# Tails of a head pair in one matmul, column tiles for the token-mix tails, a first batch mixed in channel halves, and a new order of steps

## The chip, the cores and the metric

The kernel runs on one core of a Trainium2 chip. Its time is the device time of one execution, in microseconds (us). The kernel before takes 309.3 us, the median of five runs (308.6 to 313.53).

The engines have short names here: PE is TensorE (matmuls), DVE is VectorE, ACT is ScalarE, POOL is GpSimd, and SP is SyncE, which here only issues transfers. Each works through its own list of instructions in order; semaphores hold an instruction back until its inputs and its buffers are ready.

## The reference

There are 8 batches. First comes attention with random features (8 heads, 576 positions, head size 64, 128 features), then a mixer of two two-layer networks over a width of 512:

```python
def phi(x):                                   # x: q or k, scaled
    h = einsum('bhsd,md->bhsm', x, omega) - sum(x * x, -1) / 2
    return exp(h - max(h, -1)) / sqrt(m)
kv  = einsum('bhsm,bhsd->bhmd', phi(k), v)
z   = sum(phi(k), 2)
att = einsum('bhsm,bhmd->bhsd', phi(q), kv) / (einsum('bhsm,bhm->bhs', phi(q), z) + 1e-6)
x   = att as (batch, 576, 512)
u   = x + (relu(x.T @ w_tok1) @ w_tok2).T     # token mixing, 576 -> 256 -> 576
out = u + relu(u @ w_ch1) @ w_ch2             # channel mixing, 512 -> 1536 -> 512
```

## The kernel before

**Tiling.** A batch's 576 positions are split into a main part of 512, in four tiles of 128 (`NJ`), and a tail of 64 (`ST`). All matmul operands are fp16 and sums are fp32 in PSUM. Heads go in four pairs (`hp`), since two heads' tails or two row halves of 64 fill 128 partitions.

**Attention, batch b.** `proj` computes the features of q and k of one head pair: eight matmuls of 128 columns (L338) and two of 512 (L346), all with 64 rows, so that two of them use the two row halves of the array. `proj_exp` takes the exponentials on ACT (L275). The subtraction of the row's square cancels in the quotient, apart from the k maximum: `k_max` finds a maximum per key on DVE (L362, L366), takes its reciprocal into the last column of `v_sc` and scales v with it on POOL (L374). `kv` sums keys times values over the main part in eight matmuls of 65 columns (L388) and the tail in two of 130 columns (L393). `num` and `norm` give the quotient (L414, L422, L423).

**Tails.** `k_tail` copies the 32-column tails of all heads together (L292), makes two matmuls against `bd`, a matrix with omega twice on its diagonal (L296), and one exponential. A tile of the result holds four heads in groups of 32 partitions and one of two interleaved positions, so `k_tail_max` works in four groups of 32 partitions (L317 on DVE, L318 on POOL), and `kv` needs two matmuls for a pair's 64 tail positions. `num_tail` writes the tails of two batches into the two halves of one tile `xt`.

**Mixing.** `tok1` and `tok2` are the token network, for one of two hidden tiles and one of four position tiles (L459, L462, L475). `tok2_tail` does it for the 64-position tails of two batches in four matmuls: `w2t` holds the weights twice, padded with zeros, so that one batch lands in output rows 0 to 63 and the other in 64 to 127 (L486). `u` must be transposed for the channel network: `tokT` does it on PE for batches 0 and 1 (L498), `u_write` and `load_uT` through DRAM and a transposing DMA for the others (L511, L518). `ch1` is one of twelve hidden tiles of the channel network (four matmuls of 512 columns, L530, and a relu on ACT, L537), `ch2` one of four output tiles (twelve matmuls, L542, an addition on DVE, L551, and the output transfer, L553 to L558). The collected tails of all batches are treated as a ninth batch, 8.

**Loading.** q and k of batches 0 and 1 arrive in natural layout, cast to fp16 by POOL's transfers, and are transposed on PE (`t_main` L259, `t_tail` L271, copied out at L262 and L272). From batch 2 on `cast_dram` writes a fp16 copy to DRAM (POOL's queue, L89), which `load_T_v` reads with transposing DMAs on SP's queue (L97). `load_v_all` brings v and its tail (L115, L124).

**PSUM.** There are eight banks: four for attention (`att_ps`), two for `kv` and `num` (`kn_ps`), two for mixing (`mix_ps`). A new tile of a group waits until the tile that had its bank last has been read.

**Order.** The order of all steps is a string, `order` (L569), written out by hand: the program walks through it and issues each step's instructions, each on its engine's list. Nothing reorders them afterwards. Two tables go with it: `SWAP` moves single copies or multiplications to another engine, and `HEAT` puts dummy matmuls (operand `warm`) in front of named steps at the start. The step `ch1 0 0` is the first of the channel network; `tok2 7 0` is the token network of the last batch.

Of the kernel before, what the change touches and what calls it, by code (L numbers as in the profile page):

```python
# [17 lines left out]
def kernel(  # L18
# [54 lines left out]
    HEAT = {('kv', 0, 2): 1, ('kv', 1, 0): 3, ('kv', 1, 1): 2, ('num', 0, 0): 1, ('num', 0, 3): 1, ('num', 0, 4): 1, ('num', 0, 7): 1, ('proj', 0, 1): 1, ('proj', 1, 2): 4, ('t', 0, 0, 'q'): 3, ('t', 0, 4, 'k'): 2, ('t', 0, 6, 'k'): 4, ('t', 0, 6, 'q'): 3}  # L73
    SWAP = {('c', 'q'), ('kv', 0, 3), ('kv', 1, 0), ('r1', 0, 0), ('r1', 0, 1), ('r1', 1, 1), ('t', 0, 2, 'k'), ('t', 0, 6, 'k'), ('t', 0, 6, 'q'), ('t', 1, 0, 'k'), ('t', 1, 0, 'q'), ('t', 1, 4, 'q'), ('tt', 1, 'q'), ('uT', 0, 1), ('uT', 1, 0), ('uT', 1, 1), ('uT', 1, 2), ('uT', 1, 3), ('v', 0, 2), ('v', 1, 3), None}
# [45 lines left out]
    def load_v_tail(b):  # L120
        t = ldpool.tile([P, 4, D], FP32, name="v_tail", tag="v_tail", bufs=1)
        live["vt", b] = t
        for hh in range(4):
            nc.sync.dma_start(  # L124
                out=t[32 * hh : 32 * hh + 32].rearrange("c (g w) d -> c g (w d)", g=2),
                in_=v[b, hh::4, SM:S, :].rearrange("g (c w) d -> c g (w d)", w=2),
            )
# [66 lines left out]
    w2t = wpool.tile([P, NT, 2, P], FP16, name="w2t")  # L194
# [5 lines left out]
    vz = [wpool.tile([P, 4, 4, 72], FP16, name=f"vz{i}") for i in range(2)]  # L200

    for t in (w1t, bd, *vz, *xt, w2t):
        nc.vector.memset(t, 0.0)
# [9 lines left out]
    nc.tensor.transpose(om_ps, omega_nat, ident16)  # L213
    nc.vector.tensor_copy(out=bd[0:D, 0:M], in_=om_ps[0:D, :])
# [33 lines left out]
    def t_main(b, h0, n, which):  # L248
# [18 lines left out]
    def t_tail(b, which):  # L267
        nt = live[which + "natt", b]
        ps = att_ps([P, H, ST // 2], FP16, "tt_ps")
        for h in range(H):  # L270
            nc.tensor.transpose(ps[:, h, :], nt[:, h, :], ident16[0 : ST // 2, 0 : ST // 2])  # L271
        copy_on(False, "tt", b, which)(out=live[which + "T", b][:, :, NP2:SP2], in_=ps)  # L272
# [16 lines left out]
    def k_tail(b):  # L289
        sb = live["kT", b]  # L290
        kt = apool.tile([P, H, ST // 2], FP16, name="k_tt", tag="k_tt")
        (nc.vector if b < 2 else nc.gpsimd).tensor_copy(out=kt, in_=sb[:, :, NP2:SP2])  # L292
        live["kpt", b] = apool.tile([P, 4, M], FP16, name="k_pt", tag="k_pt")
        ps = att_ps([P, 4, M], FP32, "kt_ps")
        for g in range(2):
            nc.tensor.matmul(  # L296
                ps[:, 2 * g : 2 * g + 2, :],
                kt[:, 4 * g : 4 * g + 4, :].rearrange("r h c -> r (h c)"),
                bd,
                start=True,  # L300
                stop=True,
            )
        exp(live["kpt", b], ps)

    def k_tail_max(b):
        kp = live["kpt", b]
        tmp = apool.tile([P, 4, M // 2], FP16, name="mxt", tag="mxt")
# [3 lines left out]
        mx = apool.tile([P, 4], FP16, name="kmt", tag="kmt")  # L311
        nc.vector.reduce_max(out=mx, in_=tmp, axis=AX.X)
        vs = vz[b % 2]
        for hh in range(4):
            r = slice(32 * hh, 32 * hh + 32)
            with nc.allow_low_precision(reason="fp16 operand of the matmul"):
                nc.vector.reciprocal(out=vs[r, hh, :, D], in_=mx[r])  # L317
            nc.gpsimd.tensor_tensor(  # L318
                out=vs[r, hh, :, 0:D],
                in0=live["vt", b][r],  # L320
                in1=vs[r, hh, :, D : D + 1].broadcast_to((32, 4, D)),
# [59 lines left out]
    def kv(b, hp):  # L381
# [9 lines left out]
        g, h0 = hp // 2, (hp % 2) * 2  # L391
        for w in range(2):
            nc.tensor.matmul(  # L393
                ps,
                live["kpt", b][:, 2 * g + w, :],
                vz[b % 2][:, h0 : h0 + 2, 2 * g + w, 0 : D + 1],
                start=False,
                stop=(w == 1),
            )
# [54 lines left out]
    def tok1(b, tb):  # L454
        if tb == 0:
            live["r1", b] = mpool.tile([P, NT, DM], FP16, name="r1", tag="r1")
        ps = mix_ps([P, DM], FP32, "h1_ps")
        for j in range(NJ):
            nc.tensor.matmul(  # L459
                ps, w1m[:, j, tb * P : (tb + 1) * P], live["x", b][:, j, :], start=(j == 0), stop=False  # L460
            )
        nc.tensor.matmul(  # L462
            ps, w1t[:, b % 2, tb * P : (tb + 1) * P], xt[(b // 2) % 2], start=False, stop=True
        )
        if (tb == 0) != (("r1", b, tb) in SWAP):
            nc.scalar.activation(out=live["r1", b][:, tb, :], in_=ps, func=AF.Relu)
        else:
            nc.vector.tensor_relu(out=live["r1", b][:, tb, :], in_=ps)  # L468

    def tok2(b, j):  # L470
        if j == 0:
            live["u", b] = mpool.tile([P, NJ, DM], FP16, name="um", tag="um")
        ps = mix_ps([P, DM], FP32, "ht_ps")
        for tb in range(NT):
            nc.tensor.matmul(  # L475
                ps, w2m[:, tb, j, :], live["r1", b][:, tb, :], start=(tb == 0), stop=(tb == NT - 1)
            )
        nc.vector.tensor_tensor(  # L478
            out=live["u", b][:, j, :], in0=live["x", b][:, j, :], in1=ps, op=ALU.add
        )  # L480

    def tok2_tail(pair):
        ps = mix_ps([P, DM], FP32, "htt_ps")
        for o in range(2):
            for tb in range(NT):
                nc.tensor.matmul(  # L486
                    ps,
                    w2t[:, tb, o, :],
                    live["r1", 2 * pair + o][:, tb, :],
                    start=(o == 0 and tb == 0),  # L490
                    stop=(o == 1 and tb == NT - 1),
# [3 lines left out]
    def u_transpose(src, dst, *key):  # L495
        ps = mix_ps([P, ND, P], FP16, "uT_ps")
        for db in range(ND):
            nc.tensor.transpose(ps[:, db, :], src[:, db * P : (db + 1) * P], ident16)  # L498
        copy_on(False, "uT", *key)(out=dst, in_=ps)

    def tokT(b, j):
        if j == 0:
            live["uT", b] = mpool.tile([P, ND, NJ, P], FP16, name="uT", tag="uT")
        u_transpose(live["u", b][:, j, :], live["uT", b][:, :, j, :], b, j)
# [34 lines left out]
    def ch2(c, j):  # L539
        ps = mix_ps([P, DM], FP32, "h2_ps")  # L540
        for cb in range(NCB):
# [3 lines left out]
                wc2[:, cb, :],  # L545
# [3 lines left out]
        o = opool.tile([P, DM], FP32, name="o_sb", tag="o_sb")  # L549
        u = live["u", c][:, j, :] if c < B else ut[j]  # L550
        nc.vector.tensor_tensor(out=o, in0=u, in1=ps, op=ALU.add)  # L551
        if c < B:
            nc.sync.dma_start(  # L553
                out=out[c, 0:SM, :].rearrange("(p j) d -> p j d", j=NJ)[:, j, :], in_=o
            )
        else:
            nc.sync.dma_start(out=out[2 * j, SM:S, :], in_=o[0:ST])
            nc.sync.dma_start(out=out[2 * j + 1, SM:S, :], in_=o[ST:P])  # L558
# [6 lines left out]
    def load_v_all(b):  # L565
# [4 lines left out]
        load_nat 1 0 4 k; load_nat 1 0 4 q; cast_qk k; load_nat 1 4 8 k; cast_qk q; t_main 0 0 2 q;  # L570
        load_nat_tail 1 k; t_main 0 2 2 q; t_main 0 0 2 k; t_main 0 2 2 k; t_tail 0 k; proj 0 0; proj_exp 0 0
        1; proj_exp 0 0 0; k_tail 0; load_v_tail 1; k_tail_max 0; proj_exp 0 0 2; t_main 0 4 2 k; proj_exp 0 0
        3; k_max 0 0; proj 0 1; proj_exp 0 1 2; proj_exp 0 1 0; load_nat 1 4 8 q; proj_exp 0 1 1; t_main 0 4 2
        q; t_main 0 6 2 k; proj 0 2; proj_exp 0 1 3; proj_exp 0 2 0; proj_exp 0 2 1; kv 0 0; k_max 0 1;
        proj_exp 0 2 2; num 0 0 0; t_tail 0 q; load_wtok; norm 0 0 0; t_main 0 6 2 q; kv 0 1; k_max 0 2; proj
        0 3; proj_exp 0 2 3; num 0 1 1; norm 0 1 1; proj_exp 0 3 0; proj_exp 0 3 1; cast_dram 2 k; proj_exp 0
        3 3; num 0 1 0; t_main 1 0 4 k; t_main 1 0 4 q; num 0 0 1; norm 0 1 0; proj_exp 0 3 2; q_tail 0; k_max
        0 3; kv 0 2; t_tail 1 k; proj 1 0; load_v 1; proj_exp 1 0 0; load_wc1 0; proj_exp 1 0 1; load_nat_tail
        1 q; norm 0 0 1; num 0 2 0; k_tail 1; t_main 1 4 4 k; norm 0 2 0; permute_w2 0; k_tail_max 1; kv 0 3;
        t_main 1 4 4 q; permute_w2 1; cast_dram 2 q; num 0 3 1; proj 1 1; norm 0 3 1; k_max 1 0; proj_exp 1 0  # L580
        2; proj_exp 1 0 3; proj_exp 1 1 0; proj_exp 1 1 1; num 0 3 0; num 0 2 1; proj_exp 1 1 2; norm 0 2 1;
# [113 lines left out]
```

The softmax here doesn't subtract the row's maximum and nothing guards it: scores larger than these inputs give would overflow.

## Time and profile before

| | |
|---|---|
| median of five runs | 309.3 us |
| the profiled execution | 308.6 us |
| its span, first to last instruction | 306.8 us |
| PE clock granted | 0.998 |
| DMA | 46.12 MB, 78,971 packets, mean 150 GB/s |
| instructions | 5,665 |

The span is what the profile's views cover; the profiled execution's own time is 1.8 us longer. A row of the page or of a list of groups names line, engine, operation, the tiles it writes and reads, its shape and how often it occurs; behind the bar stand busy time, mean duration in ns, and the idle time of the engine just before it with what ended it. A timeline row gives start and duration in us. Durations of matmuls are booked longer than their pace, since they overlap; what a matmul costs in a row of them is the distance between starts.

### The profile page before, as it was taken

Reading aid. Unit: us, or ns where it says so; the run is one execution under the profiler, and the core shown is the slowest. Engines: PE = TensorE matmul, PEld = TensorE weight load, DVE = VectorE, ACT = ScalarE, POOL = GpSimd, SP = SyncE. Lnnn points to the kernel's source line nnn. Section 1 sums busy time; section 2 is a strip of 40 time slices with the busy share of each in tenths; the row PEclk is TensorE's granted clock in tenths of the full one; section 3 lists DMA queues with packets and bytes.
Section 4 is the critical chain, followed back from the end, with each engine's and each line's share of the span. In section 5 each row is a group of like instructions: output and inputs, shape, how many; then the busy total and the mean of one; then the engine's idle time right before and its main releaser. Section 6 shows DMA issues by size and latency. Waiting matters only on the chain.

```text
span 306.8 us, 5665 instructions
## 1 busy us (share of the span) xinstructions
PE 290.5 (95%) x2180; PEld 143.1 (47%) x2180; DVE 162.0 (53%) x418; ACT 157.4 (51%) x305; POOL 79.3 (26%) x115
## 2 busy tenths in 40 slices
PE   6788899999999999999999999999999999999993
PEld 2454354455544544544454545545544444444441
DVE  5588984764587686446553458547733421021021
ACT  2779457944956447743673278437633134503500
POOL 9677612611261261115220042105200000000000
PEclk9999999999999999999999999999999999999999
DMA  8999989999989989987969996350232142433021
GB/s 150 187 163 158 203 119 221 227 209 163 288 129 214 269 146 193 251 163 160 213 126 177 238 247 184 91 151 25 85 109 80 71 104 101 57 91 80 2 102 69
DMA packets 78971, 46.12 MB, mean 150 GB/s; under 512 B 46816, under 2 KB 73824, under 8 KB 78560
## 3 DMA queue, kind: packets, MB, share of 16 engines
q1 hardware_dynamic: 68000, 31.50, 44.3%
q0 software_dynamic: 10672, 13.99, 28.5%
q8 instruction: 17, 0.28, 0.4%
q10 hardware_dynamic: 272, 0.26, 0.2%
q14 instruction: 10, 0.08, 0.1%
HBM read 35.88 MB, written 20.19 MB: 183 GB/s over the span
## 4 chain that ended last, share of the span: by engine, by line
PE 74%; DVE 12%; DMA 6%; POOL 2%; ACT 2%; issue 1%; SPq 1%; DVEq 0%; POOLq 0%
PE h_ps L530 28%; PE h_ps L542 26%; PE ht_ps L475 4%; PE h_ps L459 3%; DMA uT<-u 2%; DVE km L366 2%; PE num_ps L414 2%; PE k_ps L338 2%; DMA v_nat<-in_v_dram 2%; PE kv_ps L388 2%; DVE xm L423 2%; DMA q_nat<-in_q_dram 2%; DVE mx L362 2%; PE q_ps L346 2%; PE htt_ps L486 1%
## 5 line engine op out<-in xcount | busy, mean ns | idle before, releaser
L537 ACT ACTIVATE r<-h_ps 128x512 f16<-128x512 f32 x108 | 64.7, 599 | 71.8 <-PE h_ps L530 71.6
L542 PE MATMUL h_ps<-wc,r 128*128 128x512 f16 x432 | 97.0, 379 | 0.0
L530 PE MATMUL h_ps<-uT,wc 128*128 128x512 f16 x384 | 90.7, 379 | 0.6 <-DMA uT<-u 0.5
L542 PEld LDWEIGHTS <-r 128*128 128x128 f16 x432 | 41.2, 98 | 47.4 <-ACT r L537 0.3
L530 PEld LDWEIGHTS <-wc 128*128 128x128 f16 x432 | 40.0, 97 | 43.6 <-issue 2.0
L551 DVE TENSOR_TENSOR o_sb<-um,h_ps 128x512 f32<-128x512 f16 x32 | 22.0, 687 | 60.6 <-PE h_ps L542 60.5
L374 POOL TENSOR_TENSOR v_sc<-v_nat,v_sc 128x512 f16<-128x512 f32 x24 | 25.4, 1057 | 100.3 <-DVE v_sc L370 34.2
L275 ACT ACTIVATE k_p<-k_ps 128x512 f16<-128x512 f32 x64 | 37.0, 605 | 12.6 <-PE k_ps L338 10.0
L275 ACT ACTIVATE q_p<-q_ps 128x512 f16<-128x512 f32 x64 | 37.5, 604 | 4.5 <-PE q_ps L346 4.3
L478 DVE TENSOR_TENSOR um<-xm,ht_ps 128x512 f16<-128x512 f16 x32 | 21.6, 684 | 15.8 <-PE ht_ps L475 15.1
L423 DVE TENSOR_TENSOR xm<-num_ps,rc 128x256 f16<-128x256 f32 x64 | 27.2, 425 | 2.2
L318 POOL TENSOR_TENSOR vz<-v_tail,vz 32x256 f16<-32x256 f32 x32 | 20.3, 635 | 22.2 <-DVE vz L317 15.6
L366 DVE TENSOR_REDUCE km<-mx 128x8 f16<-128x512 f16 x32 | 21.9, 686 | 1.1
L475 PE MATMUL ht_ps<-r,w2m 128*128 128x512 f16 x64 | 18.9, 380 | 2.0 <-DVE r L468 1.0
L414 PEld LDWEIGHTS <-q_p 128*128 128x128 f16 x256 | 14.3, 98 | 13.6 <-issue 3.0
L362 DVE TENSOR_TENSOR mx<-k_p 128x512 f16<-128x512 f16 x32 | 16.2, 505 | 4.5 <-ACT k_p L275 4.2
L414 PE MATMUL num_ps<-kv_sb,q_p 128*128 128x65 f16 x256 | 17.0, 194 | 1.3 <-DVE kv_sb L401 1.2
L459 PE MATMUL h_ps<-xm,w1m 128*128 128x512 f16 x64 | 16.4, 380 | 0.6 <-DVE xm L423 0.6
L422 DVE RECIPROCAL rc<-num_ps 128x4 f32<-128x4 f32 x64 | 10.8, 169 | 10.5 <-PE num_ps L414 10.2
L401 ACT CAST kv_sb<-kv_ps 128x130 f16<-128x130 f32 x30 | 8.2, 272 | 14.1 <-PE kv_ps L393 14.0
L346 PE MATMUL q_ps<-qT,bd 64*128 64x512 f16 x64 | 14.4, 376 | 0.6 <-ACT q_p L275 0.3
L388 PEld LDWEIGHTS <-k_p 128*128 128x128 f16 x256 | 11.4, 98 | 6.7 <-issue 2.0
(97 smaller groups left out, 244.8 us busy)
## 6 DMA issues: line engine op xcount, KB each, us to landing
out_dram<-o_sb SPq DMA_DIRECT2D x32, 256.0 KB, 2.8
v_nat<-in_v_dram SPq DMA_DIRECT2D x12, 512.0 KB, 5.8
k<-in_k_dram POOLq DMA_DIRECT2D x6, 576.0 KB, 7.9
q<-in_q_dram POOLq DMA_DIRECT2D x6, 576.0 KB, 6.8
wc<-in_moe_w_ch_dram POOLq DMA_DIRECT2D x4, 768.0 KB, 9.2
u<-um SPq DMA_DIRECT2D x24, 128.0 KB, 2.1
v_tail<-in_v_dram SPq DMA_DIRECT2D x32, 32.0 KB, 4.5
out_dram<-o_sb SPq DMA_DIRECT2D x8, 128.0 KB, 2.3
```

Of the source, the lines that this page charges most:

```text
L275: nc.scalar.activation(out=out, in_=in_, func=AF.Exp, bias=0.0, scale=c_scale)
L362: nc.vector.tensor_tensor(out=tmp, in0=kp[:, :, 0 : M // 2], in1=kp[:, :, M // 2 : M], op=ALU.max)
L366: nc.vector.reduce_max(out=mx, in_=tmp, axis=AX.X)
L374: (nc.vector if ("v", b, hp) in SWAP else nc.gpsimd).tensor_tensor(out=vs[:, :, 0:D], in0=live["v", b][:, 2 * hp : 2 * hp + 2].rearrange(" ...
L414: nc.tensor.matmul(ps[:, j, :], live["qp", b, hp][:, j % 2, i, j // 2, :], sb, start=True, stop=True)
L423: nc.vector.tensor_tensor(out=live["x", b][:, :, h * D : (h + 1) * D], in0=ps[:, :, 0:D], in1=rc.unsqueeze(2).broadcast_to((P, NJ, D)), op ...
L459: nc.tensor.matmul(ps, w1m[:, j, tb * P : (tb + 1) * P], live["x", b][:, j, :], start=(j == 0), stop=False)
L475: nc.tensor.matmul(ps, w2m[:, tb, j, :], live["r1", b][:, tb, :], start=(tb == 0), stop=(tb == NT - 1))
L530: nc.tensor.matmul(ps, wc1[:, db, cb * P : (cb + 1) * P], uT[:, db].rearrange("p j c -> p (j c)"), start=(db == 0), stop=(db == ND - 1),)
L537: nc.scalar.activation(out=live["r3", c][:, cb, :], in_=ps, func=AF.Relu)
L542: nc.tensor.matmul(ps, live["r3", c][:, cb, j * P : (j + 1) * P], wc2[:, cb, :], start=(cb == 0), stop=(cb == NCB - 1),)
L551: nc.vector.tensor_tensor(out=o, in0=u, in1=ps, op=ALU.add)
```

## The change

Six things change.

- Key tails: the tail tile of a head pair now holds both heads and both interleaved positions (`kt`, with zeros between), against `om2`, which is omega twice, one above the other. A pair's tail is one matmul of 128 columns in `k_tail` and one of 130 columns in `kv`. `k_tail_max` works in two groups of 64 partitions. `load_v_tail` brings v in the order that goes with it.
- Token-mix tails: `tok2_tail` writes each batch to its own 64 output rows with unpadded weights, alternating between the two; `w2t` and its copies go.
- `tok1`, `tok2`, `tokT` and `ch2` can do one half of the 512 channels. The order uses it for the token mixing of batch 0 and for `ch2 8 3`.
- `t_main` and `t_tail` of batch 0 use the mixing banks instead of the attention banks.
- In the half-width `ch2 8 3 1` one of the two output transfers is issued by ACT.
- `order`, `HEAT` and `SWAP` are new throughout.

```diff
     def load_v_tail(b):
-        for hh in range(4):
+        for r in range(4):
+            i, w = r // 2, r % 2
             nc.sync.dma_start(
-                out=t[32 * hh : 32 * hh + 32].rearrange("c (g w) d -> c g (w d)", g=2),
-                in_=v[b, hh::4, SM:S, :].rearrange("g (c w) d -> c g (w d)", w=2),
+                out=t[32 * r : 32 * r + 32],
+                in_=v[b, i::2, SM:S, :].rearrange("g (c w) d -> w c g d", w=2)[w],
             )
...
-    vz = [wpool.tile([P, 4, 4, 72], FP16, name=f"vz{i}") for i in range(2)]
+    vz = [wpool.tile([P, NU, 2, 72], FP16, name=f"vz{i}") for i in range(2)]
+    kt = [wpool.tile([P, NU, 2, 2, ST // 2], FP16, name=f"kt{i}") for i in range(2)]
...
+    om2 = wpool.tile([P, M], FP16, name="om2")
+    nc.vector.tensor_copy(out=om2, in_=om_ps)
...
     def t_main(b, h0, n, which):
-        ps = att_ps([P, n, 2, P], FP16, "t_ps")
+        early = b < 1
+        ps = (mix_ps if early else att_ps)([P, n, 2, P], FP16, "t0_ps" if early else "t_ps")
...
     def k_tail(b):
-        kt = apool.tile([P, H, ST // 2], FP16, name="k_tt", tag="k_tt")
-        (nc.vector if b < 2 else nc.gpsimd).tensor_copy(out=kt, in_=sb[:, :, NP2:SP2])
+        for w in range(2):
+            r = slice(w * D, (w + 1) * D)
+            (nc.vector if b < 2 else nc.gpsimd).tensor_copy(
+                out=kt[b % 2][r, :, :, w, :],
+                in_=sb[r, :, NP2:SP2].rearrange("r (g i) c -> r g i c", i=2),
+            )
...
-        for g in range(2):
-            nc.tensor.matmul(
-                ps[:, 2 * g : 2 * g + 2, :],
-                kt[:, 4 * g : 4 * g + 4, :].rearrange("r h c -> r (h c)"),
-                bd,
+        for hp in range(NU):
+            nc.tensor.matmul(
+                ps[:, hp, :],
+                kt[b % 2][:, hp].rearrange("r i w c -> r (i w c)"),
+                om2,
...
     def k_tail_max(b):
-        for hh in range(4):
-            r = slice(32 * hh, 32 * hh + 32)
+        for i in range(2):
+            r = slice(i * ST, (i + 1) * ST)
...
     def kv(b, hp):
-        g, h0 = hp // 2, (hp % 2) * 2
-        for w in range(2):
-            nc.tensor.matmul(
-                ps,
-                live["kpt", b][:, 2 * g + w, :],
-                vz[b % 2][:, h0 : h0 + 2, 2 * g + w, 0 : D + 1],
-                start=False,
-                stop=(w == 1),
-            )
+        nc.tensor.matmul(
+            ps, live["kpt", b][:, hp, :], vz[b % 2][:, hp, :, 0 : D + 1], start=False, stop=True
+        )
...
-    def tok2(b, j):
+    def tok2(b, j, hf=None):
+        c = cols(hf)
+        ps = mix_ps([P, c.stop - c.start], FP32, "ht_ps")
...
     def tok2_tail(pair):
-        for o in range(2):
-            for tb in range(NT):
+        for tb in range(NT):
+            for o in range(2):
                 nc.tensor.matmul(
-                    ps,
-                    w2t[:, tb, o, :],
+                    ps[o * ST : (o + 1) * ST, :],
+                    w2raw[:, tb, SM:S],
                     live["r1", 2 * pair + o][:, tb, :],
-                    start=(o == 0 and tb == 0),
-                    stop=(o == 1 and tb == NT - 1),
+                    start=(tb == 0),
+                    stop=(tb == NT - 1),
                 )
...
-            nc.sync.dma_start(out=out[2 * j, SM:S, :], in_=o[0:ST])
-            nc.sync.dma_start(out=out[2 * j + 1, SM:S, :], in_=o[ST:P])
+            nc.sync.dma_start(out=out[2 * j, SM:S, d], in_=o[0:ST])
+            (nc.scalar if hf else nc.sync).dma_start(out=out[2 * j + 1, SM:S, d], in_=o[ST:P])
```

The new order, from the first half-wide token mixing to the first channel steps, and its end:

```
tok1 0 0 0; num 0 3 0; norm 0 3 0; num 0 3 1; proj_exp 1 0 3; tok1 0 1 0; proj 1 1; proj_exp 1 1 2;
cast_dram 2 q; k_tail_max 1; norm 0 3 1; num_tail 0 1; tok2 0 0 0; proj_exp 1 1 0; proj_exp 1 1 1;
tok2 0 3 0; t_tail 1 q; k_max 1 1; proj_exp 1 1 3; tok1 0 1 1; tok1 0 0 1; load_wc1 1; proj 1 2;
tokT 0 0 0; tok2 0 1 0; tok2 0 2 0; kv 1 0; tok2 0 2 1; proj_exp 1 2 2; tok2 0 0 1; kv 1 1;
proj_exp 1 2 0; tok2 0 3 1; q_tail 1; tok2 0 1 1; num 1 0 0; tokT 0 2 1; proj_exp 1 2 3; tokT 0 3 1;
tokT 0 0 1; tokT 0 2 0; proj_exp 1 2 1; tokT 0 3 0; proj 1 3; proj_exp 1 3 0; proj_exp 1 3 1;
num 1 0 1; k_max 1 2; tokT 0 1 0; tokT 0 1 1; ch1 0 0; ch1 0 5
...
tok1 1 1; ch1 0 10; k_max 2 1; tok2_tail 0; tok2 1 0; kv 2 0; tok2 1 3; num 2 0 0; tok2 1 2
...
ch1 7 1; ch1 7 10; ch1 7 7; ch1 7 11; ch2 7 3; ch2 7 2; ch2 7 1; ch2 7 0; ch2 8 3 1
```

## The prediction

> **What bounds it now.** I read the page's busy shares and slices first. They say that TensorE (PE) is nearly always busy, except in the first seventh, and that the transfers are busy for two thirds of the run.
>
> ```profile
> PE 290.5 (95%) x2180; PEld 143.1 (47%) x2180; DVE 162.0 (53%) x418; ACT 157.4 (51%) x305; POOL 79.3 (26%) x115
> PE   6788899999999999999999999999999999999993
> DMA  8999989999989989987969996350232142433021
> ```
>
> PE's busy time has modelled ends (a 512-column matmul is booked at 379 ns), so I take the pace from the chain of waits and the timeline, as distances between starts.
>
> ```profile
> 265.62 12.95 PE h_ps L542 x60
> 289.00 12.96 PE h_ps L542 x60
> 301.99 0.69 DVE o_sb L551
> ...
> 51.47 1.02 PE L530 MATMUL h_ps<-uT,wc 128*128 128x512 f16 x4
> 52.43 0.40 PE L338 MATMUL k_ps<-bd,kT 64*128 64x128 f16 x8
> 52.66 0.38 PE L346 MATMUL q_ps<-qT,bd 64*128 64x512 f16 x2
> 52.97 0.30 PE L414 MATMUL num_ps<-kv_sb,q_p 128*128 128x65 f16 x4
> ...
> 62.57 0.41 PE L388 MATMUL kv_ps<-v_sc,k_p 128*128 128x65 f16 x8
> 62.81 0.28 PE L393 MATMUL kv_ps<-vz,k_pt 128*128 128x130 f16 x2
> 62.93 0.29 PE L414 MATMUL num_ps<-kv_sb,q_p 128*128 128x65 f16 x4
> ```
>
> Prices on PE: 12.95 / 60 = 0.216 us for 512 columns; 0.24 / 8 = 0.030 for 65 columns; 0.12 / 2, about 0.058, for 130. Four matmuls of L530 cost 0.86, yet L338 comes 0.96 after them: changing the array's tiling costs about 0.095. The two 512-column matmuls of L346, in two row tiles, take 0.31 with the change back, so 0.216 for both: they run side by side.
>
> The windows split the run into three stages, with the first channel matmul (`ch1 0 0`, 43.03) as the border.
>
> ```profile
> 0.00:14.10 14.10, 9.57 (x70) 4.28 (x71) 8.32 (x30) 6.88 (x12) 11.04 (x21) 1.00 1.11 166
> 14.10:43.00 28.90, 24.76 (x305) 14.02 (x305) 24.49 (x65) 19.08 (x38) 19.02 (x29) 1.00 1.04 158
> 128.00:240.00 112.00, 112.00 (x834) 55.31 (x832) 60.18 (x158) 58.52 (x117) 23.07 (x30) 1.00 0.64 146
> 302.00:306.80 4.80, 0.00 (x0) 0.00 (x0) 0.68 (x1) 0.00 (x0) 0.00 (x0) 0.86 0.14 55
> ```
>
> (Columns: busy PE, weight load, DVE, ACT, POOL, then clock, DMA share, GB/s.) From 14.1 to 43 VectorE (DVE) is filled to 24.49 / 28.9 = 85% and ScalarE (ACT) to 66%; PE waits on them, and part of its busy time is dummies (35 `warm` matmuls in all). From 43 on PE runs. Counts by prices: 1,024 full matmuls of 512 columns x 0.216 = 221; 576 of 65 x 0.030 = 17; 64 of 130, 3.7; 128 pairs of L338 x 0.056 = 7; 32 pairs of L346, 7; 32 of 256 columns, 3.5; transposes 6; 70 tiling changes, 6.7. That is about 272 us of useful PE work; split by the listed order, 19.4 lie ahead of `ch1 0 0` and 252.6 behind it. PE ends at 301.95, so behind the border it loses 258.9 - 252.6 = **6.3 us** to waits; from 302 to 306.8 the last result goes out. So the time is: border + PE work behind it + its waits + 4.85.
>
> **The Trainium skill.** "TensorEngine Tiling (Array Packing)", Key Properties, says that tiles operate independently and that a change of mode drains the engine: the trace agrees for row tiles, with 0.095 a change. The same page, Restrictions, says that column tiling disables fast weight load; no run here shows a column tile yet. "TensorE: Matmul & The Clock Gate", Part 1, gives N / 2.4 GHz + 2.5 ns warm: 215.8 ns for 512, where the trace has 216; so I take 0.109 for 256 columns and 0.056 for 128. "DMA: Bandwidth & Descriptors", Specifications, asks for 512 B or more per transfer; the change halves the run of `load_v_tail` from 512 to 256 B, which the trace of before doesn't show for it.
>
> **The change, part by part.**
>
> *Key tails.* `kv` loses one of two 130-column matmuls, 32 times: 32 x 0.057 = **-1.8 us** of PE. `k_tail` has 4 x 0.056 for 2 x 0.109: nothing. DVE loses 16 reciprocals (16 x 0.179 = 2.9), POOL 16 of the 635 ns multiplications (10.2); both stay below PE's fill after 43, so they only give slack. `k_tail` copies in two halves of 64 partitions, as many elements per partition as the old copy (397 ns POOL, 392 DVE): between 0 (if the halves cost half) and +0.4 per batch. The exponential behind it waits that long; beside it lie `ch1` steps of 0.86, so 0. If this cover were gone: 8 x 0.4 = 3.2. The tail transfers have twice the descriptors: 32 KB, now 4.5 us to landing. Bounds 0 to +4.5 each; listed 3.9 us of PE work ahead of their use in batch 2 and 8 to 17 in the later ones, so 0.
>
> *Token-mix tails.* 16 matmuls of 0.216 become 16 of 64 output rows. Paired: 8 x 0.216 + about 6 more tiling changes x 0.095 (two of eight fall together with a projection's): 3.46 to 2.30, **-1.2**. Not paired: +0.6. Slow 64-column weight loads may add up to their booked 0.1 each, 1.6 in all. I take -1.2. Four POOL copies (0.24 each) go.
>
> *Channel halves.* The matmuls double at half width: +0.1 of PE. `ch2 8 3 1` ends the kernel: an addition of 256 columns (0.69 to about 0.4, from the 420 ns of the 256-wide `xm`) and 64 KB outputs on two queues instead of 256 KB (2.8 us to landing; the 128 KB ones have 2.3). With -0.3 and -0.5: **-0.8**; bounds -1.2 and 0 (ACT's queue idle since the start may be slower).
>
> *PE sum.* The same addition over the new list gives 2.9 us less in all (-1.8 - 1.2 + 0.1), 18.9 ahead of `ch1 0 0` and 250.3 behind: **-2.4** behind the border (252.6 to 250.3), all on the path.
>
> *Banks and order, start.* What decides is when `ch1 0 0` comes. Pricing each listed instruction ahead of it from its row: DVE 34.9 us before, 31.5 after; ACT 29.6 before, 33.0 after (copies of transposes, four half `r1`, four half `uT`). DVE is relieved by 3.4, ACT gets 3.4. The pins: q of heads 4 to 7 lands at 13.3 (weight load of L259, idle 0.71 until DMA q_nat), and these transfers keep their place on POOL's queue, so the q copies of ACT can't start before about 14.1. From there to the last `uT` copy ACT has 25.7 us listed. Without a gap that ends at 39.8; at DVE's 85% of before, at 44.4. The half-wide mixing removes just the chain norm, `tok1`, `r1`, `tok2` that left ACT idle (1.9 and 2.5 us at 35 to 38.6), and the early transposes no longer share four banks with the projections. I choose 90%: 42.5, **-0.5**, bounds -3.2 and +4.
>
> *Order, later.* Two mixing banks are refilled in turn; where a bank comes back after less PE work than its emptying needs (0.69 us on DVE for `tok2`), PE waits. Counted behind the border: four places before (1.5 us, all at `tok2 7`; the chain of waits passes through ACT's `r` there, at 242.98 and 247.81), ten after (2.2 us; `tok2 1` follows `tok2_tail 0` without a `ch1` between). **+0.7**. Bounds 0 and +2. POOL's cast of keys 6 is listed 9.4 us ahead of `proj 6 0`, but nothing slower than `k_max 5 2` stands before it on POOL, 19.6 ahead. On SP, `load_uT 3` has 6.95 us of lead (14.6 before) for 5.06 of transposes. Both hold.
>
> *Sum* against the profiled execution (span 306.8, with 1.8 around it 308.6): -0.5 - 2.4 + 0.7 - 0.8 = -3.0, so 305.6. The median of the runs, 309.3, is 0.7 above that execution, so **306.3 us**. What one measurement here can tell from no change is about 0.5%, 1.5 us.
>
> **Rivals.**
>
> *The start opens up* (0.14). ACT fills without gaps and `ch1 0 0` comes at 39.8: -5.7, 303.6. For it: ACT's idle time of before is mostly waiting on DVE, which is relieved. Against it: the first DMA-fed projection.
>
> ```profile
> 39.34 7.70 SPq L97 DMA_TRANSPOSE qT<-q  x1
> 51.95 0.39 POOL L292 COPY k_tt<-kT 128x256 f16<-128x256 f16 x1 [12.07 <-DMA kT<-k]
> ```
>
> Keys 2 landed at 51.95, 19.5 us after their q cast (32.47), 0.5 us ahead of their projection. The new list has 9.2 us of PE work between `ch1 0 0` and `proj 2 0`, so a border at 39.8 wants keys at 49.0; the q cast would have to start by 29.5.
>
> *ACT becomes the start's bound* (0.19, the slower case). It gets 25.7 us of work for a stretch where it did 19.1. If its queue, in order, stands as often as it did (its halves `r1` and `uT` wait for matmuls that wait for `um`), its fill is under 80%. At 75%: border 48.4, +5.4, so 308.6 + 5.4 - 2.4 + 0.7 - 0.8 = 311.5, median 312.2. It is break-even at 82% (border 45.5) and slower by more than 1.5 at 78%.
>
> *Gain eaten* (0.15): fill 83 to 85% and column tiles that don't pair (+1.8): 308 to 310, no difference. That the tiles don't run side by side is the case in which the change doesn't do what it says; alone it costs 1.8 and leaves 308.1.
>
> **How the numbers follow.** Forecast 0.52: 306.3, own range 304.5 to 307.7. Rival one 0.14, eaten 0.15, slower 0.19. Faster 0.66, same 0.15, slower 0.19. Range 302.5 to 311.5: it leaves out the upper half of the slower case and a start without any gap.
>
> **What would show it.** In the trace after: `htt_ps` as 128*64, two starts a few ns apart; one 130-column matmul per `kv`; the first L539 matmul (`ch1`) near 42.5; ACT over 85% busy from 14 to 42; short waits of `tok2 1`. Wrong, if `ch1 0 0` comes after 45.5, if PE waits over 2 us for keys or values of batch 2, or if its waits behind the border exceed 9 us.

## The result, and the profile after

The changed kernel takes 311.64 us (median of 43 runs, 308.79 to 317.43), the kernel before in the same series 309.92 (80 runs, 306.8 to 322.17). The ratio is **1.0069, with 1.0052 to 1.0085 as its 95% interval**: 0.7% slower, where 306.3 us was forecast. The ratios here compare undisturbed executions alone; the traces of `f1` and `g4` below come of disturbed ones, with further waits from 48 and 123 us on, so only their wait near 160 us is read.

The page of the changed kernel, its span of 308.0 us (before 306.8), busy shares, slices and the group of the channel network's first layer (`ch1`), with that group before in the last row:

```profile
PE 290.3 (94%) x2197; PEld 144.2 (47%) x2197; DVE 161.3 (52%) x411; ACT 157.8 (51%) x312; POOL 69.9 (23%) x100
PE   6789899999999999997699999999999999999995
PEclk9999999999999999999799999999999999999998
L539 PE MATMUL h_ps<-uT,wc 128*128 128x512 f16 x384 | 93.2, 383 | 5.1 <-DMA uT<-u 4.6
...
L530 PE MATMUL h_ps<-uT,wc 128*128 128x512 f16 x384 | 90.7, 379 | 0.6 <-DMA uT<-u 0.5
```

A slice is 7.7 us. PE's row has a dent at slices 19 and 20, 139 to 154 us, where the page before had nines; the clock has one at slice 20. The `ch1` group says what PE waited for: 4.6 of its 5.1 us of idle time ended with the transposing DMA into `uT` (0.5 of 0.6 before). The timeline of PE there, start and duration first:

```profile
143.37 0.81 PE L539 MATMUL h_ps<-uT,wc 128*128 128x512 f16 x3
148.77 0.38 PE L539 MATMUL h_ps<-uT,wc 128*128 128x512 f16 x1 [4.59 <-DMA uT<-u]
148.99 0.41 PE L397 MATMUL kv_ps<-v_sc,k_p 128*128 128x65 f16 x8
149.23 0.23 PE L400 MATMUL kv_ps<-vz,k_pt 128*128 128x130 f16 x1
149.29 1.03 PE L485 MATMUL ht_ps<-r,w2m 128*128 128x512 f16 x2
150.11 0.64 PE L285 MATMUL qt_ps<-qT,bd 128*128 128x256 f16 x2
150.54 2.76 PE L539 MATMUL h_ps<-uT,wc 128*128 128x512 f16 x7
```

`ch1 3 0` runs three of its four matmuls and waits for the last quarter of `uT`. And what follows is slow: from 149.3 to 152.7, in 3.4 us, the 512-column matmuls stand up to 0.427 apart instead of 0.216. Half of 3.4 is another 1.7 us lost.

Timelines of SP, DVE and POOL, and the chain of waits, say why the quarter was late:

```profile
131.02 5.99 SPq L563 DMA_DIRECT2D out_dram<-o_sb  x2
137.10 5.07 SPq L527 DMA_TRANSPOSE uT<-u  x4
...
135.93 0.69 DVE L561 TENSOR_TENSOR o_sb<-um,h_ps 128x512 f32<-128x512 f16 x1 [2.12 <-PE h_ps L552]
...
141.72 0.55 POOL L89 DMA_DIRECT2D q<-in_q_dram  x1
...
140.91 7.82 DMA uT<-u
148.77 0.38 PE h_ps L539
```

SP has two output transfers ahead of the four transposes. The second is that of `ch2 2 2`, whose result DVE has ready only at 136.6 (135.93 + 0.69), and SP stands in it. The last transpose goes out at 140.91 and lands 7.82 us later; 0.8 us after its issue POOL starts `cast_dram 7 q`. Before, SP started the same transposes at 130.46, ahead of all outputs of `ch2 2` and with no cast beside them. They landed 2.8 to 5.1 us after their issue, and `ch1 3 0` ran at 146.7. SP's timeline before, and the landing times of this reload and of the next one, which had two casts beside it (issued at 160.16 and 160.70):

```profile
130.46 5.95 SPq L518 DMA_TRANSPOSE uT<-u  x4
136.51 8.27 SPq L553 DMA_DIRECT2D out_dram<-o_sb  x4
...
DMA to landing us min/median/max: 2.8/4.2/5.1
...
DMA to landing us min/median/max: 7.0/8.9/9.7
```

So landings of 7 to 10 us beside casts were in the trace of the kernel before, too. PE never waited for that reload.

The rest of the change did what it says. Windows (columns as in the prediction), a tail of the token mixing, and the end:

```profile
14.10:41.30 27.20, 23.54 (x307) 15.59 (x307) 22.03 (x61) 21.93 (x46) 14.42 (x20) 1.00 1.13 180
...
110.81 0.71 PE L497 MATMUL htt_ps<-r,w2raw 128*64 128x512 f16 x4
111.45 0.40 PE L347 MATMUL k_ps<-bd,kT 64*128 64x128 f16 x8
...
298.75 5.36 PE L552 MATMUL h_ps<-wc,r 128*128 128x512 f16 x30
...
304.15 0.42 DVE L561 TENSOR_TENSOR o_sb<-ut,h_ps 128x256 f32<-128x256 f16 x1 [0.62 <-PE h_ps L552]
304.60 0.47 SPq L567 DMA_DIRECT2D out_dram<-o_sb  x1
304.60 0.55 ACTq L568 DMA_DIRECT2D out_dram<-o_sb  x1
```

The first `ch1` matmul comes at 41.34 (43.03 before), with ACT at 21.93 / 27.2 = 81% and DVE at 81%. This tail's four matmuls take 0.64 us to the next step, the change of tiling behind them included (0.96 before, at the tail of 191.0). From PE's end at 304.11 (298.75 + 5.36) to the end of the span it is 3.8 us, against 4.8.

### The profile page after: what moved, and what is told of

Read it like the earlier page. It is cut to its first block, busy times and chain, and to the rows that moved or that the text cites. A ratio compares the mean times of both kernels' runs of the same rounds, so it can differ in the third digit from the quotient of the medians.

```text
span 308.0 us, 5676 instructions
## 1 busy us (share of the span) xinstructions
PE 290.3 (94%) x2197; PEld 144.2 (47%) x2197; DVE 161.3 (52%) x411; ACT 157.8 (51%) x312; POOL 69.9 (23%) x100
## 4 chain that ended last, share of the span: by engine, by line
PE 82%; DVE 6%; DMA 4%; ACT 3%; POOL 2%; issue 1%; SPq 1%; POOLq 0%; DVEq 0%
PE h_ps L539 30%; PE h_ps L552 29%; PE ht_ps L485 4%; PE h_ps L467 3%; PE num_ps L417 3%; PE k_ps L347 3%; DMA uT<-u 3%; PE kv_ps L397 2%; PE q_ps L355 2%; POOL v_sc L383 1%; DMA om_f<-in_omega_dram 1%; SPq L527 1%; DVE um L488 1%; DVE km L375 1%; PE heat_ps L168 1%
## 5 line engine op out<-in xcount | busy, mean ns | idle before, releaser
L539 PE MATMUL h_ps<-uT,wc 128*128 128x512 f16 x384 | 93.2, 383 | 5.1 <-DMA uT<-u 4.6
L552 PE MATMUL h_ps<-wc,r 128*128 128x512 f16 (+1 forms) x444 | 97.0, 374 | 0.0
L552 PEld LDWEIGHTS <-r 128*128 128x128 f16 x444 | 42.3, 98 | 46.8 <-issue 0.5
L539 PEld LDWEIGHTS <-wc 128*128 128x128 f16 x432 | 39.6, 98 | 42.7 <-issue 4.3
L488 DVE TENSOR_TENSOR um<-xm,ht_ps 128x512 f16<-128x512 f16 (+1 forms) x36 | 22.0, 625 | 17.4 <-PE ht_ps L485 16.5
L426 DVE TENSOR_TENSOR xm<-num_ps,rc 128x256 f16<-128x256 f32 x64 | 27.2, 425 | 2.2
L485 PE MATMUL ht_ps<-r,w2m 128*128 128x512 f16 (+1 forms) x72 | 19.8, 362 | 1.2 <-ACT r L546 0.3
L417 PEld LDWEIGHTS <-q_p 128*128 128x128 f16 x256 | 14.1, 98 | 13.5 <-issue 4.2
L467 PE MATMUL h_ps<-xm,w1m 128*128 128x512 f16 (+1 forms) x72 | 16.8, 356 | 1.0 <-DVE um L488 1.0
L327 POOL TENSOR_TENSOR vz<-v_tail,vz 64x256 f16<-64x256 f32 x16 | 10.3, 642 | 27.1 <-DVE v_sc L379 14.1
L397 PE MATMUL kv_ps<-v_sc,k_p 128*128 128x65 f16 x256 | 12.9, 194 | 1.1 <-POOL v_sc L383 1.0
```

The source lines that it names most:

```text
L397: nc.tensor.matmul(ps[:, i, :], kp[:, j % 2, 2 * i + j // 2, :], vs[:, i * 4 + j, 0 : D + 1], start=(i + j == 0), stop=False)
L417: nc.tensor.matmul(ps[:, j, :], live["qp", b, hp][:, j % 2, i, j // 2, :], sb, start=True, stop=True)
L426: nc.vector.tensor_tensor(out=live["x", b][:, :, h * D : (h + 1) * D], in0=ps[:, :, 0:D], in1=rc.unsqueeze(2).broadcast_to((P, NJ, D)), op ...
L467: nc.tensor.matmul(ps, w1m[:, j, tb * P : (tb + 1) * P], live["x", b][:, j, c], start=(j == 0), stop=False)
L485: nc.tensor.matmul(ps, w2m[:, tb, j, :], live["r1", b][:, tb, c], start=(tb == 0), stop=(tb == NT - 1))
L488: nc.vector.tensor_tensor(out=live["u", b][:, j, c], in0=live["x", b][:, j, c], in1=ps, op=ALU.add)
```

## The experiments

Where a part is undone, the base is the changed kernel with `load_uT 3` at a better place (`e2`), since the late reload would hide it.

**`e1_uT3_early`**

```diff
-... load_v_all 5; ch1 2 11; ...; ch2 2 0; ...; ch2 2 2; ...; load_uT 3; k_tail_max 5; ch2 2 1; ...
+... load_v_all 5; load_uT 3; ch1 2 11; ...; ch2 2 0; ...; ch2 2 2; ...; k_tail_max 5; ch2 2 1; ...
```

> The changed kernel with one step moved: `load_uT 3` (four DMA transposes on SP) is listed right behind `load_v_all 5`, 16.9 us of listed PE work ahead of `ch1 3 0` instead of 6.95. Theory (the list puts the reload behind two outputs whose results SP waits for, so that it comes too late): the 4.59 us wait of PE at 148.8 goes, and with it the slow clock behind it (1.7), so 6.3 less than the changed kernel: ratio to the kernel before 1.007 - 0.020 = 0.987, with 0.983 to 0.992 as its range. Rival A (the later order is too tight for its transfers everywhere: a PE that comes 6 us earlier meets the casts of keys 6 and 7 or the next reload late): half or more of it comes back as waits after 155 us, ratio 0.997 to 1.007. Rival B (the wait is of a DMA system filled by the cast beside it, whatever the place): transposes still land 6 us or more after issue, but ahead of their use, ratio as for the theory; the landing time tells.

Measured: 304.6 us, ratio 0.9881 (0.984 to 0.9923). The wait is gone, and nothing came in its place: behind the first `ch1` matmul PE waits 6.2 us in all, as much as in the kernel before (6.3). So rival A falls. The transposes landed 2.7 to 7.1 us after issue; the slowest one ran beside `cast_dram 6 q`, as rival B has it, but with this lead it didn't matter.

**`e2_uT3_mid`** and **`g1_mid_again`**

```diff
-... ch2 2 0; ...; cast_dram 6 q; ch2 2 2; ...; k_max 5 1; proj_exp 5 1 2; load_uT 3; ...
+... ch2 2 0; ...; cast_dram 6 q; load_uT 3; ch2 2 2; ...; k_max 5 1; proj_exp 5 1 2; ...
```

> The changed kernel with `load_uT 3` just ahead of `ch2 2 2`, 10.2 us of listed PE work before `ch1 3 0`: behind the first of the two outputs on SP (`ch2 2 0`), ahead of the second. Theory (what decides is whether SP must first wait for the result of `ch2 2 2`): SP starts the transposes near 132, they end near 137.5 and land by 141 to 145, ahead of 144.2; wait under 1 us, ratio to the kernel before 0.986 to 0.992. Rival (any place behind the outputs and beside the casts is late): a wait of 2 us or more, ratio above 0.995.

> The version with `load_uT 3` just ahead of `ch2 2 2` once more, beside the three that follow, on the same chip. It had 0.9843 (0.9816 to 0.987) to the kernel before. Theory (the gain is the change's own, and the late reload was its only loss): 0.982 to 0.989 again, no wait of PE over 1 us behind the first channel matmul, which comes between 41 and 43.5. If the gain hung on one chip or on luck with the transfers: above 0.990.

Measured: 303.38 us, ratio 0.9843 (0.9816 to 0.987); on another chip 303.31 us, 0.9853 (0.9812 to 0.9894). So one step, moved past one output, turns a loss of 0.7% into a gain of 1.5%: 2.2% or 6.8 us, for which the trace of the changed kernel had 4.6 of waiting and 1.7 of slow clock. SP and PE in `g1`, timelines, and its windows at the place of the dent:

```profile
132.89 5.82 SPq L527 DMA_TRANSPOSE uT<-u  x4
138.81 4.09 SPq L563 DMA_DIRECT2D out_dram<-o_sb  x3
...
143.46 1.03 PE L539 MATMUL h_ps<-uT,wc 128*128 128x512 f16 x4
...
144.00:148.00 4.00, 4.00 (x29) 2.06 (x27) 2.27 (x5) 2.94 (x6) 0.50 (x1) 1.00 0.57 134
148.00:152.00 4.00, 4.00 (x39) 1.93 (x37) 0.49 (x1) 2.93 (x6) 1.05 (x2) 1.00 1.03 233
```

The reload starts 4.2 us earlier, the three outputs stand behind it, and `ch1 3 0` gets its four matmuls without a gap at almost the same time as in the changed kernel (143.37). This version beats both kernels.

**`e3_cast7_late`**

```diff
-... kv 5 0; tok2 4 1; cast_dram 7 q; ch1 3 0; ...; ch1 3 7; norm 5 2 1; ...
+... kv 5 0; tok2 4 1; ch1 3 0; ...; ch1 3 7; cast_dram 7 q; norm 5 2 1; ...
```

> The changed kernel with `cast_dram 7 q` moved from ahead of `ch1 3 0` to behind `ch1 3 7`; `load_uT 3` stays where the change put it. Theory (two parts: issued at 140.9, its last transpose can't land ahead of the use at 144.2, and the cast of 576 KB beside it stretches the landing from about 3.5 to 7.8 us): the landing falls to 3.5 to 4.5, the wait of PE from 4.6 to 0.3 to 1.3 us, and the clock behind it stays near 1: ratio to the kernel before 0.987 to 0.993. Rival (the landing is long by itself, because it waits behind the 256 KB outputs and the casts of batch 6): landing still above 6.5, wait above 3.3, ratio 1.000 to 1.007.

Measured: 305.06 us (303.97 to 307.73), ratio 0.9879 (0.9855 to 0.9903). The transposes went out as late as in the changed kernel (SP, L527, 137.41), but without the cast beside them they all landed in time. The list of that line, 128 to 150 us, and the chain of waits later:

```profile
DMA to landing us min/median/max: 2.7/2.8/3.3
...
163.31 9.16 DMA uT<-u
...
172.51 1.20 PE L539 MATMUL h_ps<-uT,wc 128*128 128x512 f16 x2 [3.03 <-DMA uT<-u]
```

So the late place alone made no wait at this reload; it leaves little margin, and the 576 KB cast turns that into 4.6 us. In this profiled execution, the slowest of the seven, PE lost time at the next reload instead. `load_uT 4` went out at 160.41 (158.40 in `g1`) beside `cast_dram 7 k`, which `g1` has there too; a transpose landed 9.16 us after issue, PE waited 3.0 us, and matmuls came up to 0.43 apart behind it. The other executions were 1.7 to 3.8 us faster. The median stays 1.7 us above that of `e2`; what makes that up in the other executions isn't shown.

**`e4_warm_wait`**

```diff
+        if (c, cb) == (3, 0):
+            heat(kn_ps([P, SM], FP32, "heat_ps"), "ch1", c, cb)   # 20 matmuls of `warm`
```

> The changed kernel with 20 matmuls of the `warm` tile (512 columns, 4.3 us, results unused) ahead of `ch1 3 0`, where PE waits for the reload anyway. It keeps PE busy in the wait and leaves the wait's end where it is. Theory (the slow matmuls after the wait, 427 ns apart until about 152.5, come of PE's standing idle): pitch 0.216 from the wait's end on, 1.5 to 2 us less than the changed kernel, ratio to the kernel before 1.001. Rival (the slow clock at 149 to 152.5 has another cause, such as a power limit that falls there by chance): pitch still above 0.4 there and the time as the changed kernel's or up to 0.5 us above it, ratio 1.007 to 1.009.

Measured: 309.37 us, ratio 1.0037 (1.0015 to 1.0058). The cast and the late reload are both there (one landing took 7.5 us), but PE is busy meanwhile:

```profile
144.27 4.48 PE L168 MATMUL heat_ps<-warm 128*128 128x512 f16 x20
148.59 1.16 PE L541 MATMUL h_ps<-uT,wc 128*128 128x512 f16 x4
...
148.00:152.00 4.00, 4.00 (x28) 2.00 (x27) 1.45 (x3) 2.15 (x5) 0.00 (x0) 1.00 0.47 168
...
148.00:152.00 4.00, 3.23 (x18) 1.58 (x18) 1.61 (x3) 1.85 (x4) 0.00 (x0) 0.66 0.36 128
```

The clock in 148 to 152 is 1.00 where the changed kernel, in the last row, had 0.66. Against that kernel's 1.0069 it is 0.3%, 1.0 us: somewhat under the 1.7, with another wait of 0.6 us (for `uTt`, ending at 262.6) in this trace. So the slow matmuls come of PE's standing idle. "TensorE: Matmul & The Clock Gate", Part 1, of the Trainium skill says that after an idle window of about 3.4 us the clock is at half, 426.7 ns for 512 columns. The trace agrees in the size, with 427 behind a wait of 4.59 us; but the wait of 3.03 us in `e3` brought the half clock as well, so here less than 3.4 us was enough.

**`f1_before_late`** and **`g4_before_late`** (the kernel before)

```diff
-... proj_exp 5 0 0; load_uT 3; ch2 2 0; ...; ch2 2 2; ...; ch2 2 1; ch2 2 3; ...
+... proj_exp 5 0 0; ch2 2 0; ...; ch2 2 2; ...; ch2 2 1; load_uT 3; ch2 2 3; ...
```

> The kernel before with one step moved: `load_uT 3` listed behind `ch2 2 1`, 5.7 us of PE work ahead of `ch1 3 0` instead of 14.6, so that it stands behind three outputs on SP. No other part of the change is in it. Theory (the place of this reload makes the loss, whatever else the change does): PE waits 1.7 to 6 us for `uT` at `ch1 3 0`, with a slow clock behind it if the wait is long; ratio to the kernel before 1.006 to 1.022. Rival (the old order would hide it; the loss needs the new order's earlier PE or its cast beside it): wait under 1 us, ratio 0.998 to 1.003.

> The kernel before with `load_uT 3` behind `ch2 2 1`, once more, for its trace beside a trace of the others: the first time it had 1.0182 (1.0134 to 1.0231). Theory: PE waits 2 to 6 us for `uT` at `ch1 3 0`, near 147, and matmuls come 0.43 us apart for some microseconds behind it; ratio 1.010 to 1.022. Rival (the loss lies elsewhere, such as the outputs that stand behind the reload on SP): no wait over 1 us there, whatever the ratio.

Measured: 314.71 us, ratio 1.0182 (1.0134 to 1.0231), and 316.14 us, 1.0209 (1.0143 to 1.0276). The old order doesn't hide the late reload. In `g4`'s timelines and list:

```profile
153.19 0.54 POOL L89 DMA_DIRECT2D q<-in_q_dram  x1
153.72 0.50 POOL L89 DMA_DIRECT2D k<-in_k_dram  x1
...
155.54 7.52 SPq L518 DMA_TRANSPOSE uT<-u  x4
...
163.25 2.04 PE L530 MATMUL h_ps<-uT,wc 128*128 128x512 f16 x4 [3.24 <-DMA uT<-u]
...
DMA to landing us min/median/max: 2.9/6.2/7.7
```

Again two casts start just ahead of the late transposes, landings stretch to 7.7 us, and PE stands 3.2 us (its weight load 3.6) before `ch1 3 0`. Behind it the clock is at half for another 3.4 us.

**`f2_no_col`**

```diff
-                    ps[o * ST : (o + 1) * ST, :], w2raw[:, tb, SM:S], ...
+                    ps, w2t[:, tb, o, :], ...     # zero-padded weights, one batch after the other
```

> The version with `load_uT 3` just ahead of `ch2 2 2` (0.9843 to the kernel before), with `tok2_tail` as it was: zero-padded weights `w2t`, four matmuls of 128 rows in a row, its four small POOL copies back. Theory (column tiles run side by side: the four matmuls of a tail take 0.56 in place of 0.86): 4 x 0.30 = 1.2 us slower, ratio to the kernel before 0.988. Rival (half of it is eaten, since two of the four tails are followed by 0.3 of waiting for a bank that DVE frees): 0.6 us slower, ratio 0.986; no difference would be 0.984.

Measured: 305.47 us, ratio 0.9912 (0.9879 to 0.9946). The second tail in `e2` and here, the step behind it included:

```profile
112.91 0.71 PE L497 MATMUL htt_ps<-r,w2raw 128*64 128x512 f16 x4
113.55 0.40 PE L347 MATMUL k_ps<-bd,kT 64*128 64x128 f16 x8
...
113.27 1.02 PE L501 MATMUL htt_ps<-r,w2t 128*128 128x512 f16 x4
114.23 0.40 PE L351 MATMUL k_ps<-bd,kT 64*128 64x128 f16 x8
```

From the start of the matmul ahead of it to the start of the one behind it, the four tails take 1.06, 0.79, 0.86 and 1.06 us in `e2`, and 1.08, 1.02, 1.18 and 1.16 here. So the tiles pair, but they bring 0.66 us and not 1.2, as the rival has it. The pairs are 0.237 apart instead of 0.216, which takes 0.17 over the eight. Behind the first and the last tail `tok2` starts 0.18 later than pace and tiling ask, which takes 0.36; the rival's wait for a bank fits that. From the first `ch1` to PE's last matmul it is 256.8 us here, 255.7 in `e2` and 256.3 in `g1`; the ratio's distance to them (0.6 to 0.7%, within intervals of 0.3 to 0.4% on each side) is larger than 0.66 us, and what makes the rest isn't shown.

**`f3_no_pair`**

```diff
-        nc.tensor.matmul(ps, live["kpt", b][:, hp, :], vz[b % 2][:, hp, :, 0 : D + 1], ...)
+        for w in range(2):
+            nc.tensor.matmul(ps, live["kpt", b][:, 2 * g + w, :], vz[b % 2][:, h0 : h0 + 2, 2 * g + w, ...], ...)
```

`load_v_tail`, `k_tail` and `k_tail_max` go back with it, not shown here.

> The version with `load_uT 3` just ahead of `ch2 2 2` (0.9843 to the kernel before), with the key tails as they were (`load_v_tail`, `k_tail`, `k_tail_max`, `kv` of the kernel before: two matmuls of 130 columns per head pair, four reciprocals and four POOL products per batch). Theory: 32 x 0.057 = 1.8 us of PE back; from 43 us on DVE and POOL have slack, and at the start DVE gets 8 x 0.18 = 1.4 us back ahead of the border, of which some shows: 1.8 to 3 us slower, ratio 0.990 to 0.994. Rival (POOL's longer chain to `vz`, 4 x 0.635 per batch against 1.31, makes `kv` late): over 3.5 us slower, ratio above 0.996, with PE waits on `vz`. Other rival (the removed matmuls lay beside waits): under 0.8 us, below 0.987.

Measured: 311.69 us, ratio 1.0124 (1.0077 to 1.0171): 8 to 9 us behind the base by the ratios, 5.2 by the spans (308.2 against `e2`'s 303.0). PE's own work is 1.8 up by count, and its waits for `v_sc` are 4.2 up (4.4 us in all, 0.2 in `e2`), which more than fills the rest. The list of PE's waits and the timelines of POOL and PE:

```profile
PE kv_ps L389 <- POOL v_sc L375: 4.4, 5, 1.7
...
58.15 2.83 POOL L319 TENSOR_TENSOR vz<-v_tail,vz 32x256 f16<-32x256 f32 x4 [5.68 <-DVE vz L318]
...
60.32 0.59 PE L483 MATMUL ht_ps<-r,w2m 128*128 128x512 f16 x2
62.66 0.40 PE L389 MATMUL kv_ps<-v_sc,k_p 128*128 128x65 f16 x8 [1.75 <-POOL v_sc L375]
```

The rival was right in kind, though PE waits on `v_sc` and not on `vz`: POOL's four products take 2.83 us in a row (two take 1.38 in `e2`) and make the next `v_sc` late, and so `kv`. In an order laid out for the shorter tails they aren't free. The other 3 us of the ratio aren't in this trace, which is one of the two fastest of the six executions.

**`f7_banks`**

```diff
-... ch1 6 5; norm 7 2 1; tok1 7 0; tok1 7 1; ch1 6 10; tok2_tail 3; tok2 7 0; tok2 7 3; u_write 8 3; ch1 6 9; tok2 7 2; ...
+... tok1 7 0; tok1 7 1; ch1 6 10; tok2_tail 3; ch1 6 9; tok2 7 0; ch1 6 5; tok2 7 3; ch1 6 8; u_write 8 3; tok2 7 2; ...
```

This is one of the places; `ch1` steps moved likewise around `tok2_tail 0` and ahead of `tok2 3 2`.

> The version with `load_uT 3` just ahead of `ch2 2 2` (0.9843 to the kernel before), and channel-mixing steps moved between the token-mixing steps that refill the two mixing banks at once (`ch1 0 11`, `ch1 0 10`, `ch1 0 4` around `tok2_tail 0`; `ch1 2 10` ahead of `tok2 3 2`; `ch1 6 9`, `6 5`, `6 8` around `tok2_tail 3`; `norm 7 2 1` ahead of `num_tail 7 1`). PE loses about 1.3 us to these refills at 57 to 62, 0.6 at 118 to 121 and 1.4 at 242 to 246. Theory (they are waits for a bank, covered by any matmul into the other one): 2 to 2.8 us less, ratio to the kernel before 0.975 to 0.978. Rival (DVE's rate is behind them, so they come back a step later): under 0.8 us, ratio above 0.982.

Measured: 306.48 us, ratio 0.9943 (0.991 to 0.9976): slower than its base by 0.9 to 1.0%, where 2 to 2.8 us faster was expected. The timeline at `tok2 7`:

```profile
242.69 0.59 PE L485 MATMUL ht_ps<-r,w2m 128*128 128x512 f16 x2
243.53 1.02 PE L539 MATMUL h_ps<-uT,wc 128*128 128x512 f16 x4 [0.25 <-ACT r L546]
244.39 0.59 PE L485 MATMUL ht_ps<-r,w2m 128*128 128x512 f16 x2
245.24 1.02 PE L539 MATMUL h_ps<-uT,wc 128*128 128x512 f16 x4 [0.25 <-ACT r L546]
```

Two starts of `tok2` to `ch1` are 0.85 apart, though `tok2` has 0.43 of work. With two banks in turn, the next step needs the bank of the step before `tok2`, and that one is still being read: emptying takes about 0.85 us from its last matmul, `tok2` covers 0.43. A `ch1` behind it pays the same 0.42 as another `tok2` would. So more steps in the same pair of banks don't cover such a refill; work on other banks might, and wasn't tried. In the trace PE loses 1.6 us there (1.3 in `g1`), and 0.8 more than `g1` at 48 to 64. Behind the first `ch1` it waits 2.2 us more in all; the other 1.1 us lie at 112 to 200, and their cause wasn't followed.

**`g2_no_banks`** and **`g3_whole`**

```diff
-        early = b < 1
+        early = False                                  # g2
-... tok1 0 0 0; ...; tok1 0 1 0; ...; tok1 0 1 1; tok1 0 0 1; ...; tok2 0 0 0; ...; tokT 0 1 1; ...
+... tok1 0 0; tok1 0 1; ...; tok2 0 0; ...; tokT 0 1; ...     # g3, at the later halves' places
```

> The version with `load_uT 3` just ahead of `ch2 2 2`, with the transposes of batch 0 and their dummies back in the four banks that the projections use (`att_ps` in place of `mix_ps`); order as in the change. Theory (transposes and projections then wait for each other's banks at the start): the first channel matmul 1 to 3 us later than 42.2 (the mean of five executions of the new start), ratio to the kernel before 0.988 to 0.995. Rival (the start is bound by transfers and by the work of DVE and ACT, not by banks): less than 0.5 us, ratio 0.983 to 0.987.

> The version with `load_uT 3` just ahead of `ch2 2 2`, with the first token mixing at full width: `tok1 0`, `tok2 0`, `tokT 0` once each, at the place of the later of their two halves. Theory (the halves let ACT and DVE start on heads 0 to 3 while heads 4 to 7 are still in attention; without them the chain matmul, `r1`, matmul, `u`, transpose, `uT` stands in a row again): the first channel matmul 1.5 to 3 us later than 42.2, ratio to the kernel before 0.989 to 0.994. Rival (one border is as good as the other, since batch 1's attention stands behind it): under 0.5 us, 0.983 to 0.987.

Measured: 304.6 us, 0.9877 (0.9853 to 0.9901), and 304.49 us, 0.9872 (0.9845 to 0.9899), beside 0.9853 of the base on the same chip. The first `ch1` came at 42.37 and 41.49. The new start has that matmul between 41.07 and 43.44 in seven traces (mean 41.9), so both lie within its scatter, and below what the theories asked. (In two of the seven, 42.29 and 43.44, the clock is at half for 3.4 us from about 13.5 on; the other five lie between 41.07 and 42.24, and `g2`, at full clock, 0.1 beyond them.) By the ratios each is worth about 0.2%, 0.7 us, which their intervals don't tell from nothing.

## Why the prediction was wrong

The sum by its own terms, each against the kernel before's profiled execution, for the changed kernel and for `g1`, where only the reload is moved:

| term | forecast | after | `g1` |
|---|---|---|---|
| first `ch1` matmul | -0.5 | -1.7 (41.34) | -1.9 (41.14) |
| PE work behind it (counted, 250.3) | -2.4 | -2.4 | -2.4 |
| waits behind it | +0.7 | **+6.2** (12.5) | -0.3 (6.0) |
| from PE's end to the span's end | -0.8 | -1.0 (3.8) | -1.0 (3.8) |
| sum | -3.0 | +1.1 | -5.6 |

(Waits: PE's last end, 304.11 and 297.46, less the first `ch1` less 250.3.) The spans moved by +1.2 and -5.5. By the ratio the changed kernel is 2.1 us slower; its profiled execution, 309.74 us, is one of the faster of the 43, so some 0.9 us of the loss isn't in this trace.

**The step that failed** is this one: "On SP, `load_uT 3` has 6.95 us of lead (14.6 before) for 5.06 of transposes. Both hold." It took 5.06 us, SP's time for the four transposes, as what the reload needs. From SP's start to the last landing it needed 11.6 (137.10 to 148.73), and PE waited 4.6 us. There are three points to it.

- It set the lead against the time in which SP issues the transposes. What PE waits for is the landing. The list of DMA issues before has 3.4 us as the median for `uT`. From SP's start to the last issue it is 140.91 - 137.10 = 3.8; with 3.4 that makes 7.2, more than 6.95. (In `e3` the last transpose took 2.7, and 3.8 + 2.7 was just in time.)
- The lead itself was about right: from SP's start it was 6.3 us to the first matmul of `ch1 3 0` and would have been 6.9 to the fourth. What made it short is that SP stood at the output of `ch2 2 2`. "DMA: Bandwidth & Descriptors", Anatomy of one DMA, of the Trainium skill says that a DMA's wait for a semaphore is done on the issuing sequencer ahead of dispatch; the trace agrees, with 5.99 us on SP for two outputs, the second of which had its data at 136.6. So a transfer behind an output is as late as that output's result.
- It asked of each transfer alone whether it holds. That `cast_dram 7 q` would now run beside the transposes was in the list and wasn't looked at. `e3` shows that it makes the wait: 3.3 us at most to landing without it, 7.8 and 7.5 with it (the changed kernel and `e4`). The trace of before had the size, 7.0 to 9.7 for the reload beside two casts; the median of 24 transposes hides it.

The price of such a wait isn't in the forecast either: in the trace 4.6 us of it cost 6.3, since the clock falls. The forecast named a bound beyond which it is wrong, 9 us of waits behind the border; they are 12.5.

**The other steps.** One 130-column matmul per `kv` and column tiles are in the trace as forecast. Of the 1.2 us for the tiles, `f2` leaves 0.66: 0.17 goes into the wider pairs and 0.36 into the late `tok2` behind two tails (in the table both stand under waits). The end gave 1.0 us, a little more than forecast. That the border came near 42.5 (42.7 by its own 25.7 / 0.90 + 14.1) is partly luck: ACT was filled to 81% and not 90%, which with the 25.7 us listed would have been 45.8, past the point of being wrong; but ACT's work up to the border took only 21.93 in the trace. So of the two slower rivals, ACT as the start's bound didn't come. "Gain eaten" hit the time by another mechanism: the tiles do pair. The +0.7 for refilled banks counted the ten new places and not the waits that the new order removes: three of 0.6 to 0.7 us, ending at 90.5, 111.5 and 116.4 before (between 80 and 128 us PE loses about 1.2 us less in `g1` than before). And "they only give slack" for DVE and POOL is half true: `f3` shows that this order uses POOL's slack.

What stays open: which part of the new start brings its 1.1 us on average (41.9 in seven traces, 43.0 in the one of before). `g2` and `g3` speak against the banks alone, or the halves alone, as one large cause; the two together, `HEAT`, `SWAP` and the order of loads weren't tried apart.

## What to carry to other kernels

When an order of steps is redone, follow each transfer on its own queue: when what stands ahead of it can be issued, plus its issue, plus its landing under the traffic that the new order puts beside it, against the time of its first reader. For the landing, look up what the same kind of transfer took beside the same traffic, and not its median: here 2.7 us without a cast and 7.8 beside one, where the lead was 6.9. The same list ran 1.5% faster or 0.7% slower by the place of one reload. And price a wait of TensorE of some 3 to 5 us with the slow clock behind it, here 1.7 us on 4.6.

## What the runs showed of the hardware

- Transposing DMAs of `uT` land 2.7 to 5.1 us after issue with no casting DMA beside them (`e3`, and before, at `load_uT 3`). Beside one casting DMA of 576 KB the slowest of four took 7.1 to 9.2 us (`e1`, `e4`, the changed kernel, `e3` at `load_uT 4`), beside two 7.0 to 9.7 (before, at `load_uT 4`).
- After waits of PE of 4.59 us (the changed kernel) and 3.03 us (`e3`) matmuls of 512 columns came up to 0.43 us apart instead of 0.216; in the changed kernel that lasted for 3.4 us. With 20 dummy matmuls in the wait (`e4`) the clock stayed at 1.00.
- Two column tiles of 64 output rows start 3 to 4 ns apart; pairs follow at 0.237 us for 512 columns, where single full matmuls follow at 0.216 (the changed kernel).
- A bank of PSUM written by `ch1` and read by a 0.60 us activation took the next matmul about 0.85 us after the last one into it had run (`f7`, 242.69 to 243.53).
